# Whole-batch loads of queries and keys, merged value tails, and small VectorE values kept in PSUM

## The chip, the cores and the metric

The kernel runs on one core of a Trainium2 chip, in one launch. The metric is the device time of the launch in microseconds (us). Three runs of the kernel before took 890.33, 892.95 and 894.09 us, the median being 892.95. The profile and the trace are of one further execution, which took 890.13 us; its span, from the first to the last instruction, is 888.1 us. Engines are named as in the profile: PE is TensorE, DVE VectorE, ACT ScalarE, POOL GpSimd and SP SyncE, which here issues nearly all transfers.

## What is computed

Three steps follow each other. Attention has B=8 batches, H=8 heads, S=576 positions and D=64; its result is laid out as 4608 tokens of 512 values and goes through a soft mixture of E=8 experts with 4 slots each, and the result of that through a feed-forward net of width 2048 with a squared relu. All is 32-bit in memory.

```python
scores = (q @ k.T) / sqrt(D)                       # per batch and head
scores = where(block_i >= block_j, scores, -1e9)   # blocks of 64 positions
attn = exp(scores - scores.max(-1)); attn /= attn.sum(-1) + 1e-9
x = (attn @ v).transpose(0, 2, 1, 3).reshape(4608, 512)
logits = x @ phi                                   # 32 slots
d = exp(logits - logits.max(0)); d /= d.sum(0) + 1e-9
c = exp(logits - logits.max(1)); c /= c.sum(1) + 1e-9
h = maximum((d.T @ x) @ w1[e], 0) @ w2[e]          # 4 slots of each expert e
y = c @ h
out = maximum(y @ w_in, 0) ** 2 @ w_out
```

## The kernel before

The change touches attention alone, the first 415 us or so. The work is cut into 32 pairs: pair n is batch n // 4 and the heads j and j + 4, with j = n % 4. The two heads of a pair share tiles, so that 128 rows of the array are used.

For each pair, in this order:

- **Loads** on SP. `load_pair` (L322) brings q and k in four transfers of 128 KB (L328: 128 partitions, 4 blocks, 64 values, that is pieces of 256 bytes), and for j = 0 also the last 64 positions of all heads of the batch in four of 64 KB (L335). `load_v` (L301) brings v in two of 128 KB (L306) and two tails of 16 KB (L312).
- **Scale** (`scale`, L348). ScalarE squares q and k (`junk`), a matmul sums (`ps_ssq`, L361), and VectorE turns the sums into powers of two in a chain of eight small instructions (L364 to L383) on tiles of 2 to 4 columns in SBUF.
- **Split** (`split`, L394). q and k are scaled to 16 bit: a high part by ScalarE (L413), a remainder by VectorE (L419). The keys `ka` are transposed by a transfer (L426) into `s1`; the high part of q is turned on TensorE (L435) and copied by ScalarE (L439) into `t1`.
- **Maxima** (`maxpass`, L443). Seven chunks of q k products go to PSUM (`ps_max`, L451) and are reduced by VectorE (L465). After the first five, `fin` joins the partial maxima in `mx`, a tile of nine columns in SBUF (L498, L499, L502), writes them in two parts beside the remainder of q in `qb` (L504, L507), and has `qb` transposed by a transfer (L512) into `t2`.
- **Scores** (`scores`, L519). Seven chunks (`ps_sc`, L528), each the product of `s1` and `t1` plus that of `s2` and `t2`; the second carries the remainder of q, the mask and the maximum. Half of `s2` is a copy of `s1` by a transfer (`s2copy`, L924). ScalarE takes the exponential (L566, and L548 for the last chunk).
- **Values** (`pv`). The exponentials times v (L601, L612), sums by POOL (L571), and the division.

`pair(n)` (L958) interleaves these for different pairs: scores of n, maxima of n + 2, split of n + 3, values of n - 1, and in between the logits and tokens of the batch before and the decoding of w_in (`raw` tiles, loaded at L908). The order on TensorE is that in which `pair` writes the instructions, and so is ScalarE's in the opening; on the other engines a scheduler places each instruction by its own model of when what it needs is there. Loads wait in a list `dq`; after each of the eight slots of a pair up to LR = 4 are taken from its front and issued. What is put in, and where in the list, is written in `pair`: loads of q and k for LOOK = 7 pairs ahead, of v for 2 ahead, raw tiles, and pieces of the experts' first weights (`ew`, L165).

SP issues in its order, one after the other. Each transfer uses one of eight semaphores in turn and waits until the one eight before it has landed, so at most eight are under way. PSUM has eight banks; six go round as tiles of the tag "r" (`ps_sc`, `ps_max`, `ps_qT`, `ps_ssq` and others), each free again when its last reader is done.

## Time and profile before

| | |
|---|---|
| Runs (us) | 890.33, 892.95, 894.09; median 892.95 |
| Profiled execution | 890.13 us, span 888.1 us, mean clock 0.981 |
| Busy, of the span | PE 93%, DVE 78%, ACT 71%, POOL 28% |
| Chain that ended last | PE 60%, DVE 10%, DMA 8%, POOL 8%, ACT 7%, issue 3%, SPq 2% |
| 22 to 89 us (first pairs) | PE 51.56 busy of 67 us |
| 139 to 331 us (four batches) | PE 186.50 busy of 192 us, DVE 180.83 |
| 533 to 888 us (feed-forward) | PE 349.71 busy of 355 us |

A row of busy time by stretch has the length, then the busy time of PE, of PE's weight loads (PEld), of DVE, ACT and POOL, each with its number of instructions, then the clock granted to TensorE as a share of its full speed, the share of time that the 16 DMA engines were busy, and GB/s. In a timeline or a group, `out<-in` are the program's names without numbers (`s` stands for `s1` and `s2`, `t` for `t1` and `t2`), and what stands in brackets or behind the last bar is the idle time of the engine just before and what ended it. SPq is SP's queue: its time is that of issuing, and a wait for a semaphore can be in it.

### The profile page before, as it was taken

Reading aid. Unit: us, or ns where it says so; the run is one execution under the profiler, and the core shown is the slowest. Engines: PE = TensorE matmul, PEld = TensorE weight load, DVE = VectorE, ACT = ScalarE, POOL = GpSimd, SP = SyncE. Lnnn points to the kernel's source line nnn. Section 1 sums busy time; section 2 is a strip of 40 time slices with the busy share of each in tenths; the row PEclk is TensorE's granted clock in tenths of the full one; section 3 lists DMA queues with packets and bytes.
Section 4 is the critical chain, followed back from the end, with each engine's and each line's share of the span. In section 5 each row is a group of like instructions: output and inputs, shape, how many; then the busy total and the mean of one; then the engine's idle time right before and its main releaser. Section 6 shows DMA issues by size and latency. Waiting matters only on the chain.

```text
span 888.1 us, 21999 instructions
## 1 busy us (share of the span) xinstructions
PE 823.8 (93%) x8788; PEld 612.4 (69%) x8788; DVE 691.9 (78%) x1600; ACT 627.3 (71%) x1012; POOL 248.5 (28%) x394
## 2 busy tenths in 40 slices
PE   2778999999999999979997799999999999999997
PEld 1445767676676767656532444789898988888886
DVE  5857789999999998963633899788778888888880
ACT  5467777787878786734212889987888888887770
POOL 0225747666575756573100000000000000000000
PEclk9889999999999999999999899999999999999999
DMA  8798899999997898495999500100100000000002
GB/s 165 148 167 150 166 183 191 207 177 202 173 192 165 181 151 188 97 260 188 314 388 386 210 0 1 49 25 25 42 31 25 25 24 25 25 25 24 25 25 48
DMA packets 222022, 113.18 MB, mean 127 GB/s; under 512 B 193760, under 2 KB 195808, under 8 KB 221920
## 3 DMA queue, kind: packets, MB, share of 16 engines
q1 hardware_dynamic: 219264, 111.12, 53.3%
q8 instruction: 69, 1.13, 0.5%
q10 hardware_dynamic: 2656, 0.66, 0.4%
q14 instruction: 33, 0.27, 0.1%
HBM read 78.71 MB, written 9.44 MB: 99 GB/s over the span
## 4 chain that ended last, share of the span: by engine, by line
PE 60%; DVE 10%; DMA 8%; POOL 8%; ACT 7%; issue 3%; SPq 2%; ACTq 0%; DVEq 0%
PE ps_y L1463 14%; PE ps_x L1463 9%; PE ps_z L1463 9%; PE xm L601 5%; PE po L1485 4%; POOL ss L571 4%; PE ps_hb L1427 3%; POOL ul L711 3%; DMA wch<-in_moe_w_dram 3%; PE ps_sc L528 3%; DVE pm L465 2%; DMA s<-s 2%; DMA s<-ka 2%; PE ps_h L1154 1%; PE ps_max L451 1%
## 5 line engine op out<-in xcount | busy, mean ns | idle before, releaser
L1463 PEld LDWEIGHTS <-ah 128*128 128x128 f16 x1792 | 170.4, 98 | 21.8
L566 ACT ACTIVATE p<-ps_sc,es 128x512 f32<-128x512 f32 x192 | 128.0, 692 | 40.1 <-PE ps_sc L528 25.8
L1396 DVE TENSOR_TENSOR al<-a,ah 128x1024 f16<-128x1024 f32 (+1 forms) x128 | 138.5, 1125 | 16.7 <-ACT ah L1450 15.3
L571 POOL TENSOR_TENSOR ss<-p 128x384 f32<-128x384 f32 (+1 forms) x128 | 92.8, 745 | 171.8 <-ACT p L566 171.7
L465 DVE TENSOR_REDUCE pm<-ps_max 128x4 f32<-128x512 f32 x160 | 107.1, 681 | 32.1 <-PE ps_max L459 32.0
L1450 ACT CAST ah<-a 128x1024 f16<-128x1024 f32 (+1 forms) x128 | 114.4, 936 | 15.0 <-DVE a L1396 13.6
L528 PE MATMUL ps_sc<-t,s 128*128 128x512 f16 (+3 forms) x512 | 107.1, 302 | 12.0 <-DMA s<-s 7.9
L1556 POOL TENSOR_TENSOR ot<-u,p 128x256 f32<-128x256 f32 x16 | 12.5, 782 | 374.8 <-DVE u L1527 339.4
L1463 PE MATMUL ps_y<-bh,ah 128*128 128x256 f16 x384 | 104.8, 273 | 0.0
L1463 PE MATMUL ps_y<-bl,ah 128*128 128x256 f16 x384 | 104.7, 273 | 0.0
L1463 PE MATMUL ps_y<-bh,al 128*128 128x256 f16 x384 | 104.7, 273 | 0.0
L571 POOL TENSOR_TENSOR ss<-ss,p 128x320 f32<-128x320 f32 (+1 forms) x128 | 98.1, 766 | 10.5 <-ACT p L566 1.4
L1318 ACT ACTIVATE r<-ps_hb,alpha 128x1024 f32<-128x1024 f32 x64 | 71.1, 1112 | 34.1 <-PE ps_hb L1427 33.4
L1463 PEld LDWEIGHTS <-al 128*128 128x128 f16 x896 | 87.6, 98 | 10.0
L601 PE MATMUL xm<-p,ar_hi 128*64 128x256 f32 (+3 forms) x512 | 91.6, 457 | 0.0
L1396 DVE TENSOR_TENSOR a<-a 128x256 f32<-128x256 f32 x192 | 76.2, 424 | 3.9
L1463 PE MATMUL ps_x<-bh,ah 128*128 128x256 f16 x256 | 70.1, 274 | 0.0
L1463 PE MATMUL ps_z<-bh,ah 128*128 128x256 f16 x256 | 69.9, 273 | 0.0
L1463 PE MATMUL ps_x<-bh,al 128*128 128x256 f16 x256 | 69.8, 273 | 0.0
L1463 PE MATMUL ps_z<-bl,ah 128*128 128x256 f16 x256 | 69.8, 273 | 0.0
L1463 PE MATMUL ps_x<-bl,ah 128*128 128x256 f16 x256 | 69.8, 273 | 0.0
L1463 PE MATMUL ps_z<-bh,al 128*128 128x256 f16 x256 | 69.8, 273 | 0.0
(255 smaller groups left out, 1846.5 us busy)
## 6 DMA issues: line engine op xcount, KB each, us to landing
wch<-in_moe_w_dram SPq DMA_DIRECT2D x18, 1024.0 KB, 11.1
ar_hi<-in_v_dram SPq DMA_DIRECT2D x64, 128.0 KB, 3.2
raw<-in_moe_w_in_dram SPq DMA_DIRECT2D x16, 512.0 KB, 4.9
out_dram<-ot SPq DMA_DIRECT2D x32, 256.0 KB, 2.2
ar_hi<-in_moe_w_dram SPq DMA_DIRECT2D x6, 1024.0 KB, 8.7
s<-s SPq DMA_DIRECT2D x32, 144.0 KB, 3.4
ar_lo<-in_k_dram SPq DMA_DIRECT2D x32, 128.0 KB, 3.6
ar_hi<-in_k_dram SPq DMA_DIRECT2D x32, 128.0 KB, 3.4
```

The lines of the kernel that those rows point to most:

```text
L465: nc.vector.tensor_reduce(out=o, in_=i, axis=AX.X, op=ALU.max)
L528: nc.tensor.matmul(ps[:, c0:c0 + w].rearrange("p (s c) -> p s c", c=128), kk[:, 2 * t + hp, :], qq[:, 2 * u0 + hp:8:2, :], start=(c0 == 0 ...
L566: exps[:] = [nc.scalar.activation(out=pt, in_=ps, func=AF.Exp, scale=es[:, 0:1])]
L571: add = lambda o, x, y: nc.gpsimd.tensor_tensor(out=o, in0=x, in1=y, op=ALU.add)
L601: nc.tensor.matmul(box["xm"][64 * hp:64 * hp + 64, 128 * t:512], vs[:, t, hp, :], r, start=(t == 0), stop=(t == 3),)
L711: add = lambda o, x, y: nc.gpsimd.tensor_tensor(out=o, in0=x, in1=y, op=ALU.add)
L1318: nc.scalar.activation(out=r[:, c0:c1], in_=ps[:, c0:c1], func=AF.Relu, **kw)
L1396: sub = lambda o, a, b: nc.vector.tensor_tensor(out=o, in0=a, in1=b, op=ALU.subtract)
L1427: nc.tensor.matmul(ps[:, 512 * j + 256 * a:512 * j + 256 * a + 256], ws[:, 128 * f:128 * f + 128], ctt[:, c0:c0 + 256], start=True, stop=True,
L1450: nc.scalar.copy(v(hl[n % 2][0][:, 2 * kq:2 * kq + 2], s), v(a7[n, kq], s))
L1463: nc.tensor.matmul(acc[:, 0:HM], a[:, k], b[:, k], start=bool(first and k + j == 0), stop=(k == KH - 1 and j == 2), skip_group_check=not f ...
L1485: nc.tensor.matmul(pos[t], g[:, 512 * a + 128 * t:512 * a + 128 * t + 128], tt[:, c, a], start=(c == 0 and a == 0), stop=(c == KH - 1 and ...
```

## The change

Three things are changed. First, for the batches from the third on, q and k are loaded by batch and not by pair: four tails of 64 KB as before, and eight transfers of 256 KB (`load_batch`), each of 128 positions of all eight heads. They are put at the front of `dq` in the pairs with j = 1 (tails and k) and j = 2 (q) two batches ahead. Batches 0 and 1 still use `load_pair`. Second, the tails of v come once in a batch, as two transfers of 64 KB, into two areas of their own (`v_tail`); the v tiles of the pairs shrink from 640 to 512 columns. Third, `mx` no longer has a tile in SBUF but lies in columns 0 to 8 of the PSUM bank of maxima chunk 4, and the values `a`, `hb` and `g` of the scale chain lie in the bank of `ps_ssq`; three instructions of the chain are rewritten so that each reads one value from PSUM, with their constants merged. In the changed file the lines are shifted: L306 is L309, L312 is L314, L328 is L333, L364 to L383 are L392 to L409, L419 is L445, L426 is L452, L465 is L491, L504 is L532, L507 is L535, L512 is L540, L924 is L952.

```diff
     def v_tile(n):
-        c0 = 512 * V0 + 640 * (n % 4)
-        return ar_hi[:, c0:c0 + 640].rearrange("p (a h d) -> p a h d", h=2, d=D)
+        c0 = 512 * (V0 + n % NJ)
+        return ar_hi[:, c0:c0 + 512].rearrange("p (a h d) -> p a h d", h=2, d=D)
+
+    def v_tail(b):
+        c0 = 512 * (V0 + NJ) + 256 * (b % 2)
+        return ar_hi[:, c0:c0 + 256].rearrange("p (j d) -> p j d", d=D)
...
-        mxs = [mid.tile([128, NBLK], F32, name=f"mx{i}") for i in range(2)]
...
-            def tail():
-                for h in range(2):
-                    nc.sync.dma_start(out=t[64 * h:64 * h + 64, NU, 0, :], in_=v[b][NJ * h + j, 128 * NU:S, :])
-
-            return [lambda: main(0), tail, lambda: main(1)]
+            def tail(hp):
+                nc.sync.dma_start(
+                    out=v_tail(b)[64 * hp:64 * hp + 64],
+                    in_=v[b][NJ * hp:NJ * hp + NJ, 128 * NU:S, :].rearrange("j i d -> i j d"),
+                )
+
+            return [lambda: main(0)] + [lambda hp=hp: tail(hp) for hp in range(2) if j == 0] + [lambda: main(1)]
...
+        def load_batch(b):
+            t = qk_tile(b)
+
+            def main(nm, u):
+                nc.sync.dma_start(
+                    out=t[nm][:, 2 * u:2 * u + 2].rearrange("p x j d -> p (x j) d"),
+                    in_=dict(q=q, k=k)[nm][b][:, 128 * u:128 * u + 128, :].rearrange("h p d -> p h d"),
+                )
...
+            return [
+                [lambda nm=nm, hp=hp: tail(nm, hp) for nm in "kq" for hp in range(2)],
+                [lambda u=u: main("k", u) for u in range(NU)],
+                [lambda u=u: main("q", u) for u in range(NU)],
+            ]
...
-                a, hb, g, inv = [small(nm) for nm in ("sc_a", "sc_h", "sc_g", "inv")]
+                box = lambda i: ps[:, 2 * w * i:2 * w * i + 2 * w].rearrange("p (a c) -> p a c", a=2)
+                a, hb, g = box(0), box(1), box(2)
+                inv = small("inv")
...
-                    out=sig[:, 1], in0=inv[:, 0], scalar=2.0 ** 20, in1=sig[:, 1], op0=ALU.mult, op1=ALU.min
+                    out=sig[:, 1], in0=hb[:, 0], scalar=2.0 ** 70, in1=sig[:, 1], op0=ALU.mult, op1=ALU.min
...
-                    out=inv[:, 1], in0=sig[:, 0], scalar=2.0 ** -20, in1=inv[:, 1], op0=ALU.mult, op1=ALU.max
+                    out=inv[:, 1], in0=g[:, 0], scalar=2.0 ** -71, in1=inv[:, 1], op0=ALU.mult, op1=ALU.max
...
-                    out=es[:, 0], in0=inv[:, 0], scalar=1.0 / float(D) ** 0.5, in1=inv[:, 1],
+                    out=es[:, 0], in0=hb[:, 0], scalar=2.0 ** 50 / float(D) ** 0.5, in1=inv[:, 1],
...
-            mx = mxs[n % 2]
+            box = {}
...
                 ps = ps_r.tile([128, 512], F32, tag="r", name="ps_max")
+                box[i] = ps
...
             def fin():
+                mx = box[4][:, 0:NBLK]
...
-            if n + LOOK < N:
-                at = len(dq) if n < 1 else 0
-                dq[at:at] = {0: load_pair(6), 1: load_pair(7) + load_pair(8)}.get(n) or load_pair(n + LOOK)
+            if n == 0:
+                dq += load_pair(6)
+            if n == 1:
+                dq[0:0] = load_pair(7)
+            if jn == 1 and bn + 2 < B:
+                bl = load_batch(bn + 2)
+                dq[len(load_pair(7)) if n == 1 else 0:0] = bl.pop(0) + bl.pop(0)
+            if jn == 2 and bl:
+                dq[0:0] = bl.pop(0)
```

The order of instructions on TensorE and POOL is the same as before; SP issues 392 transfers instead of 488. On SP, from the transposed queries of pair 4 (`t_1085` before, `t_1056` now) to those of pair 5 (`t_1282`, `t_1247`), the order before is this; `s_1097` are the keys of pair 6, and `s_0_141<-s_648` is the copy of pair 4:

```order
L512 DMA_TRANSPOSE t_1085<-qb_139 128x9x128
L328 DMA ar_lo<-in_q_dram 128x4x64 x2
L306 DMA ar_hi<-in_v_dram 128x4x64
L426 DMA_TRANSPOSE s_1097<-ka 128x9x128
L312 DMA ar_hi<-in_v_dram 64x64 x2
L306 DMA ar_hi<-in_v_dram 128x4x64
L924 DMA s_0_141<-s_648 64x1152
L328 DMA ar_lo<-in_k_dram 128x4x64 x2
L328 DMA ar_lo<-in_q_dram 128x4x64 x2
L306 DMA ar_hi<-in_v_dram 128x4x64
L512 DMA_TRANSPOSE t_1282<-qb_140 128x9x128
```

In the changed kernel `s_1068` are the keys of pair 6, `s_1271` those of pair 7, and `s_0_141<-s_630` is the copy of pair 4:

```order
L540 DMA_TRANSPOSE t_1056<-qb_139 128x9x128
L309 DMA ar_hi<-in_v_dram 128x4x64 x2
L952 DMA s_0_141<-s_630 64x1152
L936 DMA raw<-in_moe_w_in_dram 128x1024 x2
L452 DMA_TRANSPOSE s_1068<-ka 128x9x128
L309 DMA ar_hi<-in_v_dram 128x4x64 x2
L169 DMA ar_hi<-in_moe_w_dram 128x512 x6
L952 DMA s_1_142<-s_860 64x1152
L540 DMA_TRANSPOSE t_1247<-qb_140 128x9x128
L169 DMA ar_hi<-in_moe_w_dram 128x512 x2
L361 DMA ar_hi<-in_q_dram 64x4x64
L452 DMA_TRANSPOSE s_1271<-ka 128x9x128
```

The loads of q and k are gone from this stretch, and two raw tiles and eight pieces of the experts' weights have moved into it. The copy of pair 4 is the 93rd transfer of SP before and the 80th now, the transposed keys of pair 4 the 66th and the 62nd, the copy of pair 2 the 62nd and the 58th, and the transposed queries of pair 0 the 34th and the 35th.

In a steady batch, around the transposed keys of pair 12 (`s_2459` before), the order on SP before is this:

```order
L328 DMA ar_lo<-in_q_dram 128x4x64 x2
L306 DMA ar_hi<-in_v_dram 128x4x64
L312 DMA ar_hi<-in_v_dram 64x64 x2
L924 DMA s_0_141<-s_2002 64x1152
L306 DMA ar_hi<-in_v_dram 128x4x64
L165 DMA ar_hi<-in_moe_w_dram 128x512
L908 DMA raw<-in_moe_w_in_dram 128x1024
L512 DMA_TRANSPOSE t_2443<-qb_139 128x9x128
L426 DMA_TRANSPOSE s_2459<-ka 128x9x128
```

Now (`s_2395`):

```order
L361 DMA ar_lo<-in_q_dram 64x4x64 x2
L355 DMA ar_lo<-in_q_dram 128x8x64
L452 DMA_TRANSPOSE s_2191<-ka 128x9x128
L361 DMA ar_lo<-in_k_dram 64x4x64 x2
L355 DMA ar_lo<-in_k_dram 128x8x64 x4
L936 DMA raw<-in_moe_w_in_dram 128x1024
L540 DMA_TRANSPOSE t_2379<-qb_139 128x9x128
L452 DMA_TRANSPOSE s_2395<-ka 128x9x128
L952 DMA s_0_141<-s_1953 64x1152
```

All of the next batch's k now stands directly ahead of these keys, with the raw tile and the transposed queries.

On VectorE, where the maxima of a pair are joined and a scale chain begins, the order before is this (`mx_146`, `qb_138`):

```order
L465 TENSOR_REDUCE pm_144<-ps_max 128x4
L707 TENSOR_TENSOR ul<-ps_u,rc 128x256
L499 TENSOR_REDUCE mx_146<-pm_144 128x2x2
L184 SCALAR_TENSOR_TENSOR tin<-dec_sq,raw 128x512
L504 TENSOR_SCALAR qb_138<-mx_146 128x9
L364 TENSOR_SCALAR sc_a<-ps_ssq 128x4
L507 SCALAR_TENSOR_TENSOR qb_138<-mx_146,qb_138 128x9
```

Now:

```order
L491 TENSOR_REDUCE pm_144<-ps_max 128x4
L735 TENSOR_TENSOR ul<-ps_u,rc 128x256
L526 TENSOR_REDUCE ps_max<-pm_144 128x2x2
L188 SCALAR_TENSOR_TENSOR tin<-dec_sq,raw 128x512
L527 TENSOR_REDUCE ps_max<-pm_144 128x2x2
L392 TENSOR_SCALAR ps_ssq<-ps_ssq 128x4
L530 TENSOR_REDUCE ps_max<-ptl 128x1
L735 TENSOR_TENSOR ul<-ps_u,rc 128x256
L532 TENSOR_SCALAR qb_138<-ps_max 128x9
L393 TENSOR_SCALAR ps_ssq<-ps_ssq 128x4
L535 SCALAR_TENSOR_TENSOR qb_138<-ps_max,qb_138 128x9
```

Here the joined maxima are written to the bank `ps_max`, which its matmul used before, and ten rows stand between the reduction L491 that reads this bank last for the maxima themselves and L535, which reads it last of all. In the kernel before, the reduction L465 was the last reader.

## Rows read from the trace of the kernel before

**Rows 1.** page of the profile, parts 1 (busy) and 4 (chain)

```profile
PE 823.8 (93%) x8788; PEld 612.4 (69%) x8788; DVE 691.9 (78%) x1600; ACT 627.3 (71%) x1012; POOL 248.5 (28%) x394
...
PE 60%; DVE 10%; DMA 8%; POOL 8%; ACT 7%; issue 3%; SPq 2%; ACTq 0%; DVEq 0%
...
```

**Rows 2.** windows: stretch, length, busy by engine, clock, DMA share, GB/s

```profile
44.00:89.00 45.00, 35.76 (x506) 23.27 (x503) 27.51 (x85) 31.89 (x67) 17.03 (x25) 0.89 0.92 160
56.00:64.00 8.00, 5.79 (x57) 2.99 (x59) 2.97 (x6) 2.00 (x5) 0.00 (x0) 0.60 0.88 137
82.00:88.00 6.00, 6.00 (x78) 3.51 (x80) 3.83 (x10) 2.93 (x5) 1.43 (x2) 0.72 1.03 135
...
139.00:187.00 48.00, 46.52 (x654) 32.85 (x653) 45.27 (x117) 37.35 (x79) 31.08 (x49) 1.00 0.95 194
187.00:235.00 48.00, 46.71 (x653) 32.91 (x653) 45.01 (x116) 37.30 (x79) 31.02 (x49) 1.00 1.09 187
440.00:485.00 45.00, 39.56 (x396) 14.16 (x395) 17.51 (x77) 11.56 (x21) 0.00 (x0) 0.97 1.04 377
...
```

**Rows 3.** TensorE timeline, 22 to 89 us: start, length, line, [idle before]

```profile
32.35 0.59 PE L528 MATMUL ps_sc<-t,s 128*128 128x512 f16 x1 [3.28 <-DMA t<-qb]
...
55.09 0.39 PE L528 MATMUL ps_sc<-t,s 128*128 128x512 f16 x1 [1.07 <-DMA s<-s]
58.21 0.59 PE L451 MATMUL ps_max<-s,t 128*128 128x128 f16 x2 [2.73 <-DMA s<-ka]
...
81.72 0.39 PE L528 MATMUL ps_sc<-t,s 128*128 128x512 f16 x1 [1.07 <-DMA s<-s]
...
```

**Rows 4.** TensorE waits, 89 to 400 us: total, times, longest

```profile
PE ps_sc L528 <- DMA s<-s: 5.5, 2, 5.2
...
PE ps_max L451 <- DMA s<-ka: 1.8, 1, 1.8
...
```

**Rows 5.** timeline of SP's queue from 27 to 90 us

```profile
54.27 1.42 SPq L426 DMA_TRANSPOSE s<-ka  x1
...
78.83 0.51 SPq L924 DMA_DIRECT2D s<-s  x1
...
```

**Rows 6.** chain of waits that ended last, from 55 to 85 us, by line

```profile
by line: SPq L328 13.1%; DMA s<-ka 12.7%; SPq L426 10.1%; DMA s<-s 9.5%; SPq L512 8.6%; DMA ar_lo<-in_k_dram 8.0%; SPq L312 7.7%; SPq L306 7.3%; PE xm L601 6.9%; issue 4.1%; PE ps_max L486 3.4%; DVE qb L419 2.7%; PE ps_max L451 2.7%; SPq L9
...
```

**Rows 7.** sources L328 and L312, 20 to 130 us: ns min/median/max

```profile
L328 SPq DMA_DIRECT2D ar_hi<-in_q_dram x16: 497/506/607, 22.7 to 126.7; - x16
...
L312 SPq DMA_DIRECT2D ar_hi<-in_v_dram x20: 471/587/1037, 27.0 to 128.4; - x20
...
```

**Rows 8.** DMA issues from 20 to 130 us: count, KB each, us to landing

```profile
ar_hi<-in_moe_w_dram SPq DMA_DIRECT2D x1, 256.0 KB, 4.8
...
```

**Rows 9.** timeline of SP's queue from 130 to 240 us

```profile
194.52 3.73 SPq L426 DMA_TRANSPOSE s<-ka  x1
...
```

**Rows 10.** source L426, landing: 130 to 400 us, then 193 to 197

```profile
DMA to landing us min/median/max: 3.2/4.3/6.9
...
DMA to landing us min/median/max: 6.5/6.5/6.5
```

**Rows 11.** timeline of TensorE from 200 to 201.5 us

```profile
201.04 0.39 PE L451 MATMUL ps_max<-s,t 128*128 128x128 f16 x2
...
```

**Rows 12.** VectorE lines, 0 to 420 us: busy us, mean ns

```profile
L465 DVE TENSOR_REDUCE pm<-ps_max 128x4 f32<-128x512 f32 x160 | 107.1, 681 | 32.1 <-PE ps_max L459 32.0
...
L504 DVE TENSOR_SCALAR qb<-mx 128x9 f16<-128x9 f32 x32 | 16.5, 515 | 0.1
...
L507 DVE SCALAR_TENSOR_TENSOR qb<-mx,qb 128x9 f16<-128x9 f32 x32 | 10.8, 337 | 0.1
...
L367 DVE TENSOR_SCALAR sc_h<-sc_a 128x4 uint32<-128x4 uint32 (+1 forms) x20 | 8.8, 438 | 0.2
...
```

**Rows 13.** sources L364, L498, 0 to 420 us: ns min/median/max

```profile
L364 DVE TENSOR_SCALAR sc_a<-ps_ssq x20: 143/160/163, 11.2 to 369.9; 128x4 f32<-128x4 f32 x12, 128x2 f32<-128x2 f32 x8
...
L498 DVE TENSOR_REDUCE mx<-pm x32: 148/157/172, 26.1 to 388.1; 128x4 f32<-128x16 f32 x32
...
```

More of the change, by code (lines that the diff above doesn't have):

```diff
@@ L344, in load_pair, with tail @@
             return fs
+        def load_batch(b):
[5 more added lines that the diff above has]
+                )
+            def tail(nm, hp):
+                nc.sync.dma_start(
+                    out=t[nm][64 * hp:64 * hp + 64, 2 * NU],
+                    in_=dict(q=q, k=k)[nm][b][NJ * hp:NJ * hp + NJ, 128 * NU:S, :].rearrange("j i d -> i j d"),
+                )
+            return [
[3 more added lines that the diff above has]
+            ]
         sc = {}
@@ L361, in chain @@
                 nc.tensor.matmul(ps[:, 0:2 * w], ones[:, 0:1].to_broadcast([128, 128]), ssq.rearrange("p a c -> p (a c)"), start=True, stop=True)
-                a, hb, g, inv = [small(nm) for nm in ("sc_a", "sc_h", "sc_g", "inv")]
+                box = lambda i: ps[:, 2 * w * i:2 * w * i + 2 * w].rearrange("p (a c) -> p a c", a=2)
+                a, hb, g = box(0), box(1), box(2)
+                inv = small("inv")
                 sig, es = small("sig", bufs=4), small("es", 1, 4)
-                nc.vector.tensor_scalar(
-                    out=a, in0=ps[:, 0:2 * w].rearrange("p (a c) -> p a c", a=2), scalar1=1e-30, scalar2=None, op0=ALU.max
-                )
+                nc.vector.tensor_scalar(out=a, in0=a, scalar1=1e-30, scalar2=None, op0=ALU.max)
                 nc.vector.tensor_scalar(
@@ L612, in tl @@
                     nc.tensor.matmul(
-                        box["tl"][64 * hp:64 * hp + 64, 320:384], vs[:, t, hp if t < NU else 0, :], r,
+                        box["tl"][64 * hp:64 * hp + 64, 320:384], vs[:, t, hp, :] if t < NU else v_tail(b)[:, j, :], r,
                         start=(t == 0), stop=False,
@@ L915, in decode_in @@
             return decode(dec_p, tin[:, a, 512 * c:512 * c + 512], raws.pop(i), 512)
-        AHEAD, LOOK, LR = 3, 7, 4
+        AHEAD, LR = 3, 4
         dq = load_pair(0, dict(q=nc.scalar)) + load_pair(1, dict(q=nc.scalar)) + load_pair(2) + load_pair(3)
@@ L956, in attention @@
         ew = early = late_ = last = half = None
+        bl = []
         def pair(n):
-            nonlocal dq, work, aux, decq, ew, early, late_, last, half
+            nonlocal dq, work, aux, decq, bl, ew, early, late_, last, half
             bn, jn = divmod(n, NJ)
```

## The prediction

> **What bounds the kernel now.** I read the page first: TensorE is busy for 823.8 of 888.1 us and the chain that ends last runs 60% of the span through it [rows 1]. A change that adds no TensorE work and takes none away can win only what TensorE idles, and what it loses while its clock is down. So I cut attention into stretches [rows 2]. In steady state a batch takes 48 us, TensorE is busy in 46.5 to 46.7 of them at clock 1.00, and VectorE in 45.0 to 45.3: 1.3 to 1.5 us of idle time in a batch, and a second engine close behind. From 44 to 89 us it is different: 35.76 busy of 45 us, clock 0.89. Here are two stretches at 0.60 and 0.72, mixtures of TensorE's two levels, each around or just after a stall. The timeline names what these stalls end on [rows 3]: 3.28 us for the first transposed query (`t<-qb`), 1.07 for a copy of keys (`s<-s`), 2.73 for transposed keys (`s<-ka`), 1.07 for a copy again. From 89 to 400 us there is little such waiting [rows 4]: 5.5 us for copies, of which one, at the end of attention, is 5.2, and one of 1.8 for transposed keys.
>
> Then I asked why the transfers come late. SP's own timeline shows the keys' transpose issued at 54.27 and a copy at 78.83 [rows 5], 3.9 and 2.9 us before TensorE leaves the stalls that end on them. On the chain of waits from 55 to 85 us the lines of SP's queue lead: L328, L426, L512, L312, L306 [rows 6]. An issue of a plain load occupies SP for about half a microsecond, and one of the 16 KB value tail is no cheaper (medians 0.59 and 0.51) than one of 128 KB [rows 7]. So at the start SP's number of issues is a limit, and the DMA engines, at a share of 0.92 [rows 2], are close to being the next.
>
> **The change part by part.**
>
> *Loads.* A batch of queries and keys goes from 20 issues to 12 for six batches, 48 fewer; value tails from 8 to 2 a batch, 48 fewer. 96 x 0.55 us is 53 us of SP time, spread over attention; bytes and pieces stay. What of it lies on the path is the start. By the order the copy that ends the stall at 55.09 stands 4 issues earlier, the transpose of 54.27 also 4, and the copy of 78.83 13: 2.2, 2.2 and 7 us, if SP is all that holds them. The stalls behind these are 1.07 + 2.73 + 1.07 = 4.9 us. The slow clock costs 5.79 x 0.40 = 2.3 us in the first stretch and 6.00 x 0.28 = 1.7 in the second. The most that can come back is 8.9 us. The 3.28 us stay: the transpose they wait for now stands one issue later (price 0 to 0.6 us).
>
> But the order shows what SP's free time is filled with. Two raw tiles of 512 KB and eight pieces of 256 KB, 3 MB in all, now stand ahead of the transposed keys of pairs 6 and 7 (the order on SP); in the kernel before one such piece goes out from 20 to 130 us [rows 8]. At the 160 GB/s of this stretch 3 MB are 19 us of transfer; at the 377 GB/s that the expert stage reaches with long pieces, 8 us [rows 2]. The share of 0.92 leaves 3.6 us of 45. So between 4.4 us (8 less 3.6) and 15 us of transfer could come ahead of work that TensorE waits for; the 4 to 6.5 us between a transpose's issue and its use [rows 3, 5, 9 to 11] take up some of that. Against this stand the issues that go. I keep 5.5 of the 8.9 us (both copies, half of the keys' stall, half of the clock) and give back 2, the lower half of the 4.4: -3.5, with ends at -8.9 and +9.
>
> *Steady batches.* Here all of a batch's k and a quarter of q come in one pair, and the rest of q in the next, in loads of 256 KB, instead of four of 128 KB in every pair. The tight transfer is the transposed keys: one issued at 194.52 takes 6.5 us and TensorE starts on it at 201.04, so with no spare time at all; the median is 4.3, the shortest 3.2 [rows 9 to 11]. Counted in the order, the seven issues ahead of one of a batch's four such transposes now hold 1888 KB (288 of queries, 512 raw, 1024 and 64 of k) where there were at most 1360 in the batches up to 190 us; ahead of the other three 1232 to 1472, much as before. If all of that is still under way, 528 KB more at 194 GB/s are 2.7 us; in proportion to the queueing seen (6.5 less 3.2, by 528/1360) 1.3 us. But the transpose waits for VectorE too, and there the change helps (next part). I take 0; ends: -1.3 us a batch, all of TensorE's idle time, and +1.3 to +2.7, each for six batches.
>
> *Small values in PSUM.* L504 takes 515 ns on the mean, L507 337, L367 438 [rows 12], though they write 9 columns or fewer; L364, which reads PSUM, takes 160 in the median on 2 to 4 columns, and never more than 163 [rows 13]. If the three fall to 160, VectorE saves 32 x 0.355 + 32 x 0.177 + 20 x 0.278 = 22.6 us over attention, 2.8 a batch (the chain's other lines are shorter and left out). TensorE is the busier of the two, so nearly all of this is off the path. I take 0 and count it against the lateness of the keys.
>
> This rests on one inference: that L364 is short because its source lies in PSUM. The reductions L498 read SBUF and are as short, 148 to 172 ns, so it may be the kind of instruction instead; then nothing is saved. The ends are 0 and 22.6 us of VectorE.
>
> [...]
>
> *Banks.* The bank of chunk 4 is now held until L507's successor has read it. By the order some nine other VectorE rows stand between its own reduction and that; at 0.16 us for the small ones and 0.68 for a large reduction [rows 12, 13] that is 2 to 4 us longer. Six banks go round, and scores and maxima alone take 14 in a pair's 12 us, so a bank is wanted again some 5 us after it was taken. Price 0 to 1 us a pair; from 89 to 400 us no wait of TensorE for VectorE stands among its waits [rows 4], so I take 0, the nearer end.
>
> *The end of attention.* The 5.2 us stall [rows 4] stays: the copy of pair 30 still stands behind two weight loads. One load of 1 MB now stands ahead of the last transposed queries; 0 to +2 us, taken as 0.
>
> Sum: -3.5 + 0.3 = -3.2 us on the profiled execution, which is 890.13 us (span 888.1), so 886.9. The median of the runs shown, 892.95, is 2.8 above it, so the same change there gives 889.7; I say 887.
>
> **The rivals.**
> 1. *No give-back.* The DMA engines take the weights in their gaps, the start gains all 8.9 us and VectorE's relief half of the idle time, 6 x 0.65 = 3.9. Time 877. For it: the share rises to 1.09 in a steady batch [rows 2], so 0.92 is not a ceiling. Against: bytes move at no more than 194 GB/s there.
> 2. *Nothing moves.* What SP saves is waited for at the DMA engines; start and batches within 1 us. Time 890 to 892. For it: share 0.92 to 1.09 all through attention.
> 3. *Slower: keys behind deep queues.* Eight transfers are under way at a time, now of up to 256 KB; the transposed keys land after their use. Price 1.3 to 2.7 us for one pair of each of six batches, and nearly as much again by the clock (2.3 us after the stall of 2.73), 14 to 30 us; with half of the lower end and the start's gain lost, about +8: 898. It decides where the landing takes over 6.5 us. For it: [rows 9 to 11]. Against: the loads are issued early in a pair, the transpose late, and VectorE frees 2.8 us a batch for it.
> 4. *Slower: banks.* 0.3 us a pair, 32 pairs: 897. For it: six banks, VectorE at 94%. Against: [rows 4] names no such wait.
>
> **How the numbers follow.** Forecast 0.40 (882 to 890), rival 1 0.16, rival 2 0.21, rival 3 0.17, rival 4 0.06. What a measurement tells from no change is 0.5%, 4.5 us, so faster is below 888.5. Faster: 0.16 + 0.8 x 0.40 = 0.48. Slower, above 897.4: 0.6 of rivals 3 and 4 and a tail of the others (0.07) = 0.21. Same: 0.31. The range takes in rival 1 and the middle of rival 3: 873 to 901.
>
> **What will show it.** Right: no stall of 1 us for `s<-s` at 55 and 82, a clock above 0.95 from 44 to 89, successors of L504 and L507 at 150 to 200 ns, the batch at 48 us. Rival 3: waits of TensorE for `s<-ka` in every batch, with medians of landing above 5 us. Rival 4: TensorE waiting for VectorE's `qb`. The weights: larger landing times from 70 to 110 us, and a stall there. The prediction is wrong if a steady batch changes by over 1 us, or if the start loses time.

## The result: 1.1% slower, and the profile after

The changed kernel took 901.25 us (median of four runs, 896.72 to 905.91), the kernel before 892.33 beside it (890.33 to 894.09). The ratio is 1.0112 with a 95% interval from 1.008 to 1.0144. I had said 887, with a range up to 901. The profiled execution took 901.67 us; its span is 899.9 us.

The page's busy times answer to [rows 1]:

```profile
PE 831.6 (92%) x8788; PEld 614.9 (68%) x8788; DVE 668.6 (74%) x1600; ACT 627.2 (70%) x1012; POOL 254.8 (28%) x394
...
```

VectorE has 23.3 us less work, TensorE 7.8 more with the same instructions: part of its time was at the lower clock (0.50 from 170 to 173 us, for one; the mean was 0.973 for 0.981). To place the loss I used the start of each pair's last exponential (`pd`, in ScalarE's timeline) and cut the span with it: the start up to pair 8, the steady batches from pair 8 to 24, the end from 24 to 31, and the rest.

| us | start to pair 8 | pairs 8 to 24 | pairs 24 to 31 | span |
|---|---|---|---|---|
| before | 139.27 | 192.24 | 92.37 | 888.1 |
| changed | 141.98 | 203.87 | 90.12 | 899.9 |

So 11.6 of the 11.8 us lie in the steady batches, where I had taken 0; the start lost 2.7, the end won 2.3, and the rest is 0.3 shorter. Stretches of the changed kernel, in the columns of [rows 2]: the first pairs, a steady batch, and two short stretches in it and later:

```profile
44.00:89.00 45.00, 36.07 (x460) 22.20 (x456) 24.65 (x85) 30.00 (x63) 17.47 (x25) 0.85 1.02 191
139.00:187.00 48.00, 45.40 (x594) 31.46 (x593) 41.02 (x115) 34.75 (x73) 31.97 (x48) 0.96 0.83 158
166.00:174.00 8.00, 6.03 (x40) 2.92 (x39) 7.70 (x20) 3.15 (x7) 3.46 (x5) 0.79 0.67 139
317.00:326.00 9.00, 5.56 (x27) 2.20 (x27) 7.25 (x19) 2.77 (x7) 2.91 (x4) 0.68 0.82 181
...
```

The steady batch has a clock of 0.96 where it had 1.00, with stretches of 0.79 and 0.68. Each follows a stall; these are the changed kernel's, from TensorE's timeline (L556 was L528, L477 was L451):

```profile
33.92 0.58 PE L556 MATMUL ps_sc<-t,s 128*128 128x512 f16 x1 [4.30 <-DMA t<-qb]
...
56.87 0.58 PE L477 MATMUL ps_max<-s,t 128*128 128x128 f16 x2 [1.92 <-DMA s<-ka]
...
70.82 0.46 PE L556 MATMUL ps_sc<-t,s 128*128 128x512 f16 x1 [2.02 <-DMA s<-s]
...
169.09 0.39 PE L556 MATMUL ps_sc<-t,s 128*128 128x512 f16 x1 [1.81 <-DMA ar_hi<-in_v_dram]
...
220.03 0.39 PE L556 MATMUL ps_sc<-t,s 128*128 128x512 f16 x1 [1.86 <-DMA s<-s]
...
270.22 0.39 PE L556 MATMUL ps_sc<-t,s 128*128 128x512 f16 x1 [0.99 <-DMA ar_hi<-in_v_dram]
...
321.18 0.61 PE L556 MATMUL ps_sc<-t,s 128*128 128x512 f16 x1 [3.44 <-DMA s<-s]
...
411.95 0.39 PE L556 MATMUL ps_sc<-t,s 128*128 128x512 f16 x1 [4.04 <-DMA s<-s]
```

Four times, once a batch, the second product of a pair's scores waits: it needs the copy of keys, of pairs 11, 15, 19 and 23. (Two of the waits are put down to a load of v beside it; that product reads no v, and the copies landed at 169.05 and 270.17, 0.05 us or less ahead of its start.) These pairs took 3.2, 3.4, 0.8 and 5.7 us longer than before, for stalls of 1.81, 1.86, 0.99 and 3.44. The transposed keys, which I had named as the tight transfer, have no stall there.

SP's queue shows why. First the changed kernel, then the kernel before, both from the transposed queries of pair 11 to the copy of pair 11, and before a little past it:

```profile
155.79 2.56 SPq L540 DMA_TRANSPOSE t<-qb  x1
158.40 0.58 SPq L309 DMA_DIRECT2D ar_hi<-in_v_dram  x1
159.02 0.63 SPq L314 DMA_DIRECT2D ar_hi<-in_v_dram  x1
159.75 1.75 SPq L452 DMA_TRANSPOSE s<-ka  x1
161.55 0.60 SPq L314 DMA_DIRECT2D ar_hi<-in_v_dram  x1
162.25 0.55 SPq L936 DMA_DIRECT2D raw<-in_moe_w_in_dram  x1
162.85 0.42 SPq L309 DMA_DIRECT2D ar_hi<-in_v_dram  x1
163.32 1.34 SPq L952 DMA_DIRECT2D s<-s  x1
```

```profile
154.56 1.76 SPq L512 DMA_TRANSPOSE t<-qb  x1
156.37 0.63 SPq L924 DMA_DIRECT2D s<-s  x1
157.04 2.32 SPq L328 DMA_DIRECT2D ar_lo<-in_k_dram  x2
159.46 1.48 SPq L426 DMA_TRANSPOSE s<-ka  x1
```

Before, the copy is the next issue behind the queries; now six issues stand between. One of these is the transposed keys of pair 13, which waited for VectorE until 161.17, 1.4 us after SP turned to them; another is a raw tile of 512 KB. Pair 10 ended (its `pd`) at 164.49 before and at 166.76 now, so the copy was issued 8.1 us ahead of its use and now 3.4. The landing of this one copy (its line alone, in the changed kernel and before):

```profile
DMA to landing us min/median/max: 5.7/5.7/5.7
```

```profile
DMA to landing us min/median/max: 4.0/4.0/4.0
```

In the changed kernel the copies of pairs 11, 15, 19 and 23 landed 2.3, 2.3, 1.5 and 3.9 us behind the end of the pair ahead of them; before, 4.2 to 7.8 us ahead of it.

The small values got as short as I had said. The lines that answer to [rows 12] (L532 was L504, L535 L507, L393 L367):

```profile
L535 DVE SCALAR_TENSOR_TENSOR qb<-ps_max,qb 128x9 f16<-128x9 f32 x32 | 6.2, 193 | 0.1
L532 DVE TENSOR_SCALAR qb<-ps_max 128x9 f16<-128x9 f32 x32 | 6.0, 187 | 0.1
...
L393 DVE TENSOR_SCALAR ps_ssq<-ps_ssq 128x4 uint32<-128x4 uint32 (+1 forms) x20 | 3.4, 171 | 0.2
...
```

### The profile page after: what moved, and what is told of

Read it like the earlier page. It is cut to its first block, busy times and chain, and to the rows that moved or that the text cites. A ratio compares the mean times of both kernels' runs of the same rounds, so it can differ in the third digit from the quotient of the medians.

```text
span 899.9 us, 21874 instructions
## 1 busy us (share of the span) xinstructions
PE 831.6 (92%) x8788; PEld 614.9 (68%) x8788; DVE 668.6 (74%) x1600; ACT 627.2 (70%) x1012; POOL 254.8 (28%) x394
## 4 chain that ended last, share of the span: by engine, by line
PE 64%; DMA 11%; POOL 8%; ACT 8%; DVE 4%; SPq 3%; issue 3%; ACTq 0%; DVEq 0%
PE ps_y L1498 14%; PE ps_x L1498 9%; PE ps_z L1498 9%; PE xm L629 6%; PE po L1520 4%; POOL ss L599 4%; DMA s<-s 4%; POOL ul L739 3%; PE ps_hb L1462 3%; PE ps_sc L556 3%; DMA wch<-in_moe_w_dram 3%; DMA ar_hi<-in_v_dram 2%; ACT p L594 2%; PE tl L640 2%; ACT t L465 1%
## 5 line engine op out<-in xcount | busy, mean ns | idle before, releaser
L491 DVE TENSOR_REDUCE pm<-ps_max 128x4 f32<-128x512 f32 x160 | 108.5, 683 | 58.2 <-PE ps_max L485 57.9
L599 POOL TENSOR_TENSOR ss<-p 128x384 f32<-128x384 f32 (+1 forms) x128 | 95.0, 763 | 176.4 <-ACT p L594 176.0
L556 PE MATMUL ps_sc<-t,s 128*128 128x512 f16 (+3 forms) x512 | 107.4, 302 | 21.3 <-DMA s<-s 11.4
L599 POOL TENSOR_TENSOR ss<-ss,p 128x320 f32<-128x320 f32 (+1 forms) x128 | 101.2, 791 | 11.8 <-ACT p L594 3.1
L629 PE MATMUL xm<-p,ar_hi 128*64 128x256 f32 (+3 forms) x512 | 97.6, 481 | 0.0
```

What stands on the lines that cost most here:

```text
L491: nc.vector.tensor_reduce(out=o, in_=i, axis=AX.X, op=ALU.max)
L556: nc.tensor.matmul(ps[:, c0:c0 + w].rearrange("p (s c) -> p s c", c=128), kk[:, 2 * t + hp, :], qq[:, 2 * u0 + hp:8:2, :], start=(c0 == 0 ...
L599: add = lambda o, x, y: nc.gpsimd.tensor_tensor(out=o, in0=x, in1=y, op=ALU.add)
L629: nc.tensor.matmul(box["xm"][64 * hp:64 * hp + 64, 128 * t:512], vs[:, t, hp, :], r, start=(t == 0), stop=(t == 3),)
```

## The experiments

Theory A: the scheduler, with q and k by batch, sets two copies of keys in each batch later on SP, and they land behind their use. Rival B: PSUM banks held longer. Rival C: the depth of the queue, with 256 KB loads, whatever the order. All times are medians. The ratio is to the kernel before on the same chip, with its 95% interval; it need not be the quotient of the two medians. The runs were made on several chips, so differences of medians between rows are good to a microsecond or two. The columns of stretches are of one profiled execution each, and those of e13, e14 and e8 took 5.5 us less, 5.3 more and 4.7 more than their medians.

| run | time, us | ratio | start to 8 | 8 to 24 | 24 to 31 |
|---|---|---|---|---|---|
| e1 PSUM values only | 892.95 | 1.0008 (0.9983 to 1.0033) | 136.68 | 199.28 | 93.00 |
| e2 q, k by batch only | 900.07 | 1.0074 (1.0050 to 1.0098) | 144.03 | 195.01 | 93.16 |
| e3 value tails only | 887.41 | 0.9952 (0.9930 to 0.9974) | 137.81 | 194.52 | 90.19 |
| e14 all but q, k by batch | 884.96 | 0.9918 (0.9892 to 0.9944) | 139.66 | 195.22 | 91.67 |
| e4 changed, copies early | 882.24 | 0.9868 (0.9838 to 0.9899) | 138.81 | 191.06 | 84.89 |
| e5 before, copies early | 885.38 | 0.9925 (0.9898 to 0.9951) | 141.53 | 193.66 | 84.48 |
| e6 changed, early from pair 4 | 884.43 | 0.9919 (0.9891 to 0.9946) | 142.47 | 190.97 | 85.35 |
| e7 changed, early 8 to 24 | 892.79 | 0.9998 (0.9968 to 1.0028) | 143.22 | 190.96 | 91.33 |
| e8 changed, 128 KB pieces | 884.46 | 0.9918 (0.9889 to 0.9948) | 142.82 | 190.99 | 90.49 |
| e13 before, copies late | 892.61 | 1.0011 (0.9990 to 1.0032) | 137.74 | 194.57 | 91.15 |
| e9 changed, weights held | 896.21 | 1.0049 (1.0024 to 1.0073) | 136.74 | 206.35 | 90.22 |
| e10 both e4 and e9 | 881.83 | 0.9881 (0.9851 to 0.9911) | 139.10 | 190.95 | 85.45 |
| e12 as e10, not pair 3 | 884.41 | 0.9915 (0.9882 to 0.9949) | 142.51 | 191.19 | 85.10 |
| e11 e14 with copies early | 878.46 | 0.9848 (0.9815 to 0.9882) | 134.40 | 192.59 | 85.23 |

**One part at a time (e1, e2, e3, e14).** The diffs are against the changed kernel, and shortened. e1 takes back the loads:

```diff
-                bl = load_batch(bn + 2)
+                dq[at:at] = ... load_pair(n + LOOK)
-            return [lambda: main(0)] + [... tail(hp) ... if j == 0] + [lambda: main(1)]
+            return [lambda: main(0), tail, lambda: main(1)]
```

> Only the third part of the change: maxima and scale-chain values in PSUM, with the loads of the kernel before (488 transfers on SP). Theory A (the loss comes from the copies of keys, which the scheduler sets later on SP once q and k come by batch): here the copies stand where they stood before, so no new wait of TensorE for them, and VectorE's successors of L504 and L507 fall to 150 to 200 ns; 888 to 893 us, a gain of 0 to 4 us against the kernel before. Rival B (PSUM banks held longer stall TensorE): 895 us or more, with small waits of TensorE for VectorE or ScalarE in every batch. Rival C (deep queues of 256 KB loads): as A here, since these loads are not in it.

e2 takes back the tails and the PSUM values, e3 the loads of q and k and the PSUM values, e14 the loads of q and k alone:

```diff
-                mx = box[4][:, 0:NBLK]
+                mx = mxs[n % 2]
-                a, hb, g = box(0), box(1), box(2)
+                a, hb, g, inv = [small(nm) for nm in ("sc_a", "sc_h", "sc_g", "inv")]
```

> Only the first part: q and k by batch in 256 KB loads from the third batch on; value tails by pair and small values in SBUF as before (440 transfers on SP). Theory A: the order has the copies of two pairs of each batch behind the raw load and the values' loads, as in the changed kernel, so the whole loss is here: 898 to 904 us, with stalls of 1 to 3.5 us for the copy in one pair of each batch. Rival B: 890 to 893 us. Rival C: the loss as in A.

> Only the second part: the tails of v in two transfers of 64 KB a batch, q and k by pair and small values in SBUF as before (440 transfers on SP). Theory A and rival C: the copies keep their place, 48 issues fewer; 889 to 893 us. Rival B: the same, 892 us. If fewer issues on SP are by themselves enough to move the copies back, it is slower, 896 us or more.

> Value tails by batch and small values in PSUM, q and k by pair as before, no priority changed (440 transfers on SP): the changed kernel less its first part. In its order the copies stand as early as in the kernel before. Theory A: the loss is gone and the small gains of the two other parts stay, 884 to 890 us; the stall at the end of attention stays, so it is 6 to 9 us above the same kernel with early copies (878). If the three parts together displaced the copies, and not the first, 898 us or more.

The PSUM values alone move nothing that can be measured, the value tails alone win 0.5%, both together 0.8%; so neither B nor fewer issues by themselves are the loss. (In its profile e1 lost 7.0 us in the steady batches, most of it behind four waits for transposed keys, 6.4 us in all, and won 2.6 at the start; theory A had not said so. In e14 one such wait, of 2.41 us, made pair 12 4.3 us longer than in the kernel e4 below. The transfer that the prediction feared does stall TensorE, but in the kernels with loads by pair.) The loads of q and k by batch cost 8.3 us alone and 16.3 on top of the other two (medians, the second across chips). In e2 the copies stood late as in the changed kernel, and stalled every batch, but for a shorter time; here are two of them, and the stretch of the first:

```profile
171.13 0.39 PE L555 MATMUL ps_sc<-t,s 128*128 128x512 f16 x1 [1.27 <-DMA s<-s]
...
317.16 0.39 PE L555 MATMUL ps_sc<-t,s 128*128 128x512 f16 x1 [1.52 <-DMA s<-s]
```

```profile
168.00:175.00 7.00, 5.73 (x74) 3.76 (x75) 7.00 (x19) 4.34 (x10) 5.20 (x6) 1.00 0.70 149
...
```

The clock of these stretches stayed at 1.00, and e2's steady batches lost 2.8 us and not 11.6. The rest of its loss is at the start (4.8), where I had not expected it of this run.

**The copies early (e4, e7, e6, e5).** One edit, with a bound on n in the three last (`8 <= n < 25`, `n >= 4`, and `n >= 4` on the kernel before):

```diff
-        s2copy = lambda n: nc.sync.dma_start(out=s2[n % NB2][0:64], in_=T[n][1][0:64])
+        def s2copy(n):
+            with tc.high_priority():
+                nc.sync.dma_start(out=s2[n % NB2][0:64], in_=T[n][1][0:64])
```

> The changed kernel with one thing more: the copies of keys are given to the scheduler with high priority, so that on SP each stands about where it stood before (the copy of pair 11 directly behind the transposed queries of pair 11, that of pair 10 within the loads of k). All sizes and all 392 transfers stay. Theory A: the stalls for the copies at one pair of each batch vanish and with them the time at half clock, 8 us or more: 887 to 894 us. Rival C (the depth of the queue, not the place): copies still land 4 to 6 us after their issue and TensorE still waits; 898 us or more. Rival B: no change, 901 us.

> The changed kernel with high priority for the copies of pairs 8 to 24 alone; start and end keep their order. Theory A: what the steady batches lost to late copies in the profile (3.2 at pair 11, 3.4 at 15, 0.8 at 19, 5.7 at 23, less the 1.8 won at 25) comes back, 11 us, and the stall at the end and that at the start stay: 889 to 893 us. Rival C (queue depth): the time stays at 898 us or more.

> The changed kernel with high priority for the copies from pair 4 on, not for the first four. With all copies early, the copy of pair 3 stood at the head of SP's queue and waited there for TensorE, and the transposed keys of pair 4 behind it came 5.2 us late. Theory A: that stall falls to the 1.9 us of the changed kernel; 877 to 881 us against 882. If the start has other limits (the DMA engines), it stays at 882.

> The kernel before with only the copies of keys from pair 4 on given high priority. Theory A says that the place of the copy is what counts. In the steady batches its copies already stood early, so nothing changes there (48.0 us a batch); at the end of attention the copy of pair 30 should move ahead of the two weight loads, and the 5.2 us stall with its slow clock (together 7 to 9 us) goes: 882 to 886 us. If it is the new loads and PSUM values that make the changed kernel with early copies fast, this one stays at 889 to 893 us.

e4 took 19 us from the changed kernel with all its sizes and transfers kept, and e7, which moves the steady copies alone, 8.5; in their profiles the steady batches got 12.8 and 12.9 us shorter. e7 is the clean test: its orders on VectorE, ScalarE and POOL are those of the changed kernel, and on SP only one transposed queries and one load of v in each batch change their place besides the copies. C falls: in e4 the eight copies of the third and fourth pairs landed no sooner after their issue (3.8 to 5.5 us, 4.5 on the mean, against 4.3 in the changed kernel), but 7.7 us or more ahead of the pair's end. Its waits of TensorE from 139 to 331 us name no transfer, and its clock is back at 1.00:

```profile
PE ps_max L513 <- DVE x L844: 2.6, 4, 0.7
PE ps_x L834 <- DVE pm L491: 0.9, 4, 0.2
PE ps_sc L565 <- ACT p L594: 0.7, 4, 0.2
```

```profile
139.00:187.00 48.00, 46.68 (x657) 33.19 (x654) 42.26 (x118) 37.91 (x80) 32.26 (x49) 1.00 0.96 175
164.00:172.00 8.00, 7.34 (x119) 5.25 (x118) 7.74 (x22) 5.90 (x15) 3.07 (x5) 1.00 0.56 112
...
```

e5 shows the same edit winning 0.75% on the kernel before, and it wins it at the end (92.37 to 84.48 us): there the copy of pair 30 passes the weight loads. The 7.9 us are near to the stall of 5.2 us and half of the 4 us after it in which TensorE was busy at clock 0.50 (399.5 to 403.5 us in the kernel before), 7.2 by this estimate. At e7's start and end nothing was won, as expected. The expectation for e6 was wrong: the stall at the keys of pair 4, 5.2 us in e4, fell to 2.8, but TensorE waits 3.25 us for the copy of pair 3, and nothing is gained.

**The size of a load (e8).** The order changed with it: the copies stood early again.

```diff
-                    out=t[nm][:, 2 * u:2 * u + 2].rearrange("p x j d -> p (x j) d"),
+                    out=t[nm][:, 2 * u + x],
```

> The changed kernel with each 256 KB load of q or k as two of 128 KB, at the same places in the list of loads (440 transfers on SP, the same bytes); no priority is changed. In its order the copy of pair 11 stands directly behind the transposed queries and one load, that of pair 10 within the loads of k, as in the kernel before. Theory A: no steady stalls for the copies, 887 to 893 us. If it is the grouping of a batch's loads in two pairs that costs time, and not the copies' place, then 898 us or more.

The same bytes in the same pairs of a batch, and the steady batches take 190.99 us. The grouping of the loads is not the cause. Nor does this run show that the size is: the order changed with it, and e4 has the same steady batches with 256 KB. (e3, e4 and e8 came out 2 to 5 us faster than the ranges expected for theory A.)

**The copies late in the kernel before (e13).** A dependency that only sets the order ties them behind the transposed keys:

```diff
+            if 10 <= n < 24 and n % 4 in (2, 3):
+                tc.add_manual_dep(x.ins, lastS[-1].ins.name, ...)
```

> The kernel before, unchanged but for the order on SP: the copies of the third and fourth pair of a batch (10, 11, 14, 15, 18, 19, 22, 23) are tied behind the transposed keys that SP issues in the same pair, about where the changed kernel has them. Loads of 128 KB, values in SBUF, 488 transfers. Theory A (the place alone): issued some 3.5 us before the end of the pair before, landing after 3.4 to 4 us or more, so stalls of 0.5 to 2 us in one or two pairs of each batch and as much again at half clock: 896 to 903 us. If late copies cost only together with the deep queue of 256 KB loads, it stays at 891 to 894 us.

This went against the theory as I had put it. The copies were issued 1.7 to 5.9 us ahead of the pair's end, seven of the eight within 4.3 us of it as in the changed kernel (2.3 to 3.8), but landed at most 1.7 us behind it. Two stalls came of it, at pairs 15 and 19:

```profile
213.72 0.39 PE L529 MATMUL ps_sc<-t,s 128*128 128x512 f16 x1 [1.34 <-DMA s<-s]
...
262.47 0.39 PE L529 MATMUL ps_sc<-t,s 128*128 128x512 f16 x1 [1.42 <-DMA ar_hi<-in_v_dram]
```

```profile
211.00:218.00 7.00, 5.66 (x83) 3.64 (x84) 7.00 (x17) 4.18 (x9) 4.75 (x6) 1.00 1.16 202
260.00:266.00 6.00, 4.58 (x53) 2.64 (x52) 6.00 (x15) 3.26 (x8) 4.39 (x6) 1.00 1.27 173
...
```

The clock held, the steady batches lost 2.3 us and the whole nothing that can be measured (the profiled execution was the fastest of twelve). Of the 2.3 us the two pairs took 1.3; 1.1 is at pair 9, at a wait for transposed keys. So the late place is necessary for the loss (e4, e7, e8) and not sufficient: in the changed kernel the four copies that TensorE waits for landed 5.2 to 6.4 us after their issue, the eight here 2.8 to 5.9, and after its longer stalls the clock was lower (0.79, 0.81 and 0.68 after 1.81, 1.86 and 3.44 us).

The traces show what stood ahead of the slow copies. In the changed kernel each of those four was issued 1.1 us behind a raw tile of 512 KB and landed 1.5 to 2.3 us behind that tile; the four of pairs 10, 14, 18 and 22, issued 5 us or more behind one, landed 2.7 to 3.1 us after their issue. e13 has both cases in one run. The copy of pair 11, with no raw tile in the 15 us ahead of it, and that of pair 15, directly behind one, and their landings:

```profile
160.58 0.59 SPq L926 DMA_DIRECT2D s<-s  x1
161.27 0.53 SPq L909 DMA_DIRECT2D raw<-in_moe_w_in_dram  x1
...
208.13 0.56 SPq L909 DMA_DIRECT2D raw<-in_moe_w_in_dram  x1
208.75 0.49 SPq L926 DMA_DIRECT2D s<-s  x1
```

```profile
DMA to landing us min/median/max: 2.8/2.8/2.8
...
DMA to landing us min/median/max: 4.9/4.9/4.9
```

The copies of pairs 15 and 19 stand directly behind a raw tile, and these two stalled TensorE; those of 11 and 23 do not, and did not. That a late copy costs most where a raw tile is just ahead of it is read from these rows; no run moved the raw tile alone.

**The weights held back (e9, e10, e12).** Raw tiles and single weight pieces are tied in the order to the last exponential ahead of them; e12 leaves the copy of pair 3 without priority:

```diff
-            nc.sync.dma_start(
+            after_exp(nc.sync.dma_start(
                 out=raw.rearrange("p f x -> p (f x)"),
...
+            if n != 3:
```

> The changed kernel, with the raw tiles and the single pieces of the experts' weights tied in the order to the last exponential before them, so that the 3 MB no longer stand ahead of the transposed keys of pairs 6 and 7 but come one piece a pair, as in the kernel before. The copies keep their late places in the steady batches. If the 3 MB delay the start, as the prediction had it (2 us given back, up to 9), then pair 8 ends earlier than 141.98 us by 2 us or more: 896 to 899 us. Theory A alone, with the start lost to the late copy of pair 3: no earlier than 141 us at pair 8, and 900 to 902 us.

> The changed kernel with both: all copies of keys at high priority, and the raw tiles and weight pieces held back as in the run before. If the 3 MB cost nothing while the copies are early: 881 to 884 us, as with early copies alone (882). If they cost 2 us or more at the start: 877 to 880 us.

> As the run with early copies and held weights, but the copy of pair 3 without high priority, since at the head of SP's queue it made the transposed keys of pair 4 wait behind it (a stall of 5.2 us). Theory: that stall falls under 3 us, the copy of pair 3 comes 1 to 3 us late instead; 877 to 882 us, at best 4 us under the run with all copies early. If the start is bound by the DMA engines, no difference to that run.

By 130 us nine pieces of weights had gone out in the changed kernel, three in e9:

```profile
ar_hi<-in_moe_w_dram SPq DMA_DIRECT2D x9, 256.0 KB, 5.7
...
```

```profile
ar_hi<-in_moe_w_dram SPq DMA_DIRECT2D x3, 256.0 KB, 3.3
...
```

e9's pair 8 ends 5.2 us earlier, and its time is 5 us lower. With early copies the same edit gains nothing (e10 against e4); but in e4 the priority had by itself put both raw tiles behind the transposed keys of pair 6 and six of the eight pieces behind those of pair 7, so this pair of runs does not test the weights. e12 against e6 is nearer to a test: in both the copy of pair 3 is late and the later ones early, in e6 all nine pieces stand ahead of the keys of pair 7, and besides the weights only the priority of the first three copies differs. They took 884.41 and 884.43 us, with pair 8 at 142.51 and 142.47: no cost of the weights shows there. e12 lost 2.6 us to e10, where I expected a gain: the stall at the keys of pair 4 fell from 5.5 to 2.6 us as expected, but the copy of pair 3 then cost 3.3.

**The best version (e11).** q and k by pair, value tails by batch, values in PSUM, copies early:

> All copies of keys at high priority, value tails by batch and small values in PSUM, but q and k loaded by pair as in the kernel before (440 transfers on SP). Theory A: with the copies early the grouping of q and k decides little; 880 to 885 us. If the loads by batch are themselves worth what they were made for, fewer issues at the start, this one is slower than early copies with them (882): 885 us or more. If they cost something beside the copies' place, it is faster: 879 us or less.

878.46 us is 1.5% under the kernel before, 2.5% under the changed one, and below the 880 to 885 us that theory A gave; e14 puts 6.5 us of it down to the copies' priority. In the profiles that wins 6.4 us at the end, 5.3 at the start and 2.6 in the steady batches, of which the last two are uncertain, since e14's profiled execution was its slowest. With the copies early, the loads by batch are no gain that shows: e4 has 882.24, on another chip, and the intervals of the two ratios overlap. The steady batches are shorter with them (191.06 us in e4, 192.59 here), the start longer (138.81, 134.40).

## Why the prediction was wrong, step by step

- *Steady batches, taken as 0: the step that failed.* I asked which transfer has the least time to spare in the kernel before, found the transposed keys [rows 9 to 11], and priced those alone. They landed 1.4 us earlier on the mean of pairs 10 to 25, relative to the pair's end. The copies, which landed 4 us or more ahead, were issued 4 to 8 us later through the order, again relative to the pair's end. The order in front of the prediction shows it: among the rows around the keys of pair 12, the copy (`s_0_141<-s_1953`) has come behind the raw tile, the queries and the keys. I had counted the copies' places at the start only, where they moved forward. The 6.5 us of the transposed keys were also misread as queueing: [rows 9] has 3.73 us of them as the issue itself, in which SP waited for VectorE until 198.18, and they landed 2.7 us after it. Measured: +11.6 us, 13.1 of longer pairs 11, 15, 19 and 23, less small gains elsewhere.
- *Rival 3* had nearly the right time (898 for 901) and part of the right condition, landings too slow for their use, but the wrong transfer, and a queue's depth as the cause; that its time was near is luck. Depth without the late place cost nothing (e4: 191.06 us for the steady batches, 192.24 before), the late place in the kernel before nothing that can be measured (e13: ratio 1.0011).
- *The start, -3.2:* it lost 2.7 us. The copies for pairs 2 and 4 came early as counted (the stalls of 1.07 at 55 and 82 us are gone), that for pair 3 did not: it stalls for 2.02, and pair 3 took 3.6 us longer. The wait for the first transposed queries grew from 3.28 to 4.30, and the clock from 44 to 89 us was 0.85 and not above 0.95. The 3 MB of weights were named, with 2 us; e9 puts them at 5.2 us while all copies keep the changed kernel's places, inside the bounds that I gave, and e12 against e6 shows none once the copies from pair 4 on are early.
- *Small values in PSUM:* 0 for the time was right (e1: 1.0008). Of VectorE's work 22.6 us were forecast from three lines, and these saved 20.5 (36.1 to 15.6, [rows 12] and above). That all of VectorE lost 23.3 is near to the forecast by luck: the chain's other lines, left out of it, saved 10.7 more, and other instructions, the decoding of w_in above all (3.7 us), took longer. PSUM as a source is not what a short time needs: in the kernel before, L504, with all operands in SBUF, took 178 ns on the mean in the 3 instructions that met no POOL work and 550 in the 29 that did. The changed instructions take 149 to 193 ns. L504 fell from 515 to 187 ns and L507 from 337 to 193, while two reductions of the same values (L498, L499) took 158 and 157 before and 168 now; L380, with two inputs in SBUF, took 146 to 153 before, beside POOL or not. So some lines were long beside POOL and others were not, and no run shows what decides which.
- *Banks, 0:* e4 has about 1.05 us of small waits for VectorE and ScalarE in a batch, where the kernel before had 1.0 for ScalarE. Right in size. (Nine rows stand between the two in the order on VectorE, as the prediction counts, not ten.)
- *The end:* the stall stayed, as said (4.04 for 5.18). That it could be removed by one priority I did not see; it was worth more than the whole change.
- *The sum:* the median less 3.2 us gives 889.7, as the prediction says; for the 887 that it then names it gives no reason. That is not what made it wrong.

Open: why the changed kernel's late copies landed more slowly than those of e2 (5.2 to 6.4 us against 3.8 to 4.3) with the same loads of q and k. The traces show one difference: they were issued 1.1 us behind the raw tile, those of e2 2.3 to 2.6, and both landed 1.5 to 2.3 us behind it. Open too is what makes the start differ by up to 10 us between kernels (134.40 to 144.03) in single executions. Neither was tested.

## What to carry to other kernels

When a change frees an in-order issue queue, the scheduler refills it: list every transfer that TensorE waits for in the steady loop, and compare for each how far ahead of its use it stood and now stands, not only the one that is tightest today. A transfer with a fixed deadline should get its place by priority or by an explicit order, not by what happens to be around it; here that was worth 19 us on the changed kernel. Look also at what is issued just ahead of it. And price a stall with its clock: the waits for late copies in e2, e13 and the changed kernel cost from next to nothing (0.75 us in e2) to 1.8 times their length.

## What the runs showed of the hardware

A stall's price was not its length. After idle times of 1.27, 1.34 and 1.42 us the granted clock of the stretch stayed at 1.00, full speed (e2, e13), and e2's pair 11 took only 0.6 us longer than before; after 1.81 and 3.44 us it was 0.79 and 0.68 in stretches of 8 and 9 us, and the pairs took 3.2 and 5.7 us longer. Those shares are mixtures of two levels: the changed kernel's clock was 1.00 from 168 to 170 us and 0.50 from 170 to 173, and the records of it and of the kernel before hold no third value. A wait of 1.8 us for transposed keys in the kernel before ([rows 4], at 333 us) left the clock at 1.00 too:

```profile
333.00:340.00 7.00, 6.51 (x111) 4.74 (x112) 5.88 (x13) 3.85 (x10) 2.90 (x5) 1.00 1.08 262
```

Its pair took 1.8 us longer than the same pair of a batch in e4, which does not wait there. So nearly equal idle times, 1.77 and 1.81 us, were followed by different clocks, and the runs do not show what decides it.

In the changed kernel and e13 the copies of keys (144 KB) of pairs 10, 11, 14, 15, 18, 19, 22 and 23 landed 2.7 to 3.5 us after their issue where no load of 512 KB was issued in the 5 us ahead of them, and 4.9 to 6.4 us close behind one; close behind two loads of 256 KB such a copy took up to 5.5 us (e4, pair 19). Two VectorE instructions on nine columns took 187 and 193 ns with one operand in PSUM (L532 and L535), and 515 and 337 with all in SBUF (L504 and L507), where POOL was at work beside 29 of the 32 of each; the three of each that met no POOL work took 178 and 189 with all in SBUF.
